# Later sequences carry one running log sum, and their decay columns go

## The chip, the cores and the metric

The kernel runs on one core of one Trainium2 chip. The metric is device time in microseconds (us). The kernel before takes 425.86 us as the median of three runs (425.14 to 426.12).

## What is computed

For 4 sequences of 768 tokens, 8 heads of 48 features, a gated linear attention runs first. A state S decays with a complex factor a(t) per feature, takes in k v', and is read by q. A gated MLP with a spatial product follows on the attention's output x.

```python
scale = np.minimum(mag, 0.999) / (mag + 1e-06)        # mag = |a|
for t in range(S):
    new_re = ar * S_re - ai * S_im
    new_im = ar * S_im + ai * S_re
    S_re, S_im = (new_re + kv, new_im)
    y[:, :, t] = np.einsum('bhd,bhde->bhe', q[:, :, t], S_re)
...
h = gelu(x @ w_in);  u, v = halves of h
v_s = np.einsum('ts,bsd->btd', w_sg, layernorm(v) * g_ln) + b_sg[None, :, None]
return x + (u * v_s) @ w_out
```

a_re is drawn from 0.85 to 0.95.

## The kernel before, in words

The attention is done in chunks of 128 tokens: 6 for each sequence, 24 in all, called a0 to a23. The decay is turned into factors on q and k: q is multiplied by exp(+half the sum of the log magnitudes since the chunk began), k by exp of minus that, and both by a cosine and a sine. Then a chunk is a masked product (weigh, L662, gives pa; causes, L672, gives am), a state product (ps, L694) and the output (py, L719 and L724). Because the sums begin anew in each chunk, the state S has to be multiplied by the chunk's whole decay when it passes to the next one: L705 in a sequence's first chunk, L707 (add) and L710 (multiply) in the later ones.

The factors are prepared for a unit of 1 or 2 chunks at a time. The first sequence (units 0 to 3) is laid out with tokens on the partitions. The three later ones (units 4 to 12, the test is `fea(n)`) have features on the partitions and use scans along the tokens. For such a unit:

- `logs` (chain g, L407) ends in two scans of 384 columns (L448 to L450). They multiply by `going`, which is 0 at each chunk's first token, so that the sum restarts there.
- `scale` (chain e, L453) makes em and ep (the exponentials), multiplies k and q, and then makes the unit's decay columns `dec`: a DVE product `cols_` (L499), six small fp32 matmuls into `pd` (L507; each is issued as two records, so a block is 12), and a copy to SBUF by `evac` (L510).
- `turns` (chain p, L518) scans the angles. Those scans already carry over from unit to unit by the small tile `left` (L536).
- `rotate` (chain r) multiplies by cosine and sine and writes to DRAM (rk, rq); `heads` (chain z) reads them back as K and Q tiles.

The MLP of a sequence has the chains n (`normal`: load x, split it into xh and xl, product pv, gelu, norm, split into vh and vl), x (`expand`: product pu) and y (`spatial`: products pvs and po). Chain w prepares weights, h and k only check input ranges, l, m and v load inputs, o sets constants up, s takes sine and cosine.

The whole order of work is written out by hand in `ORDER` (L32 to L85). A token such as `a5` runs chain a5 up to its next `yield`; `a5:2` runs two steps, one or two primes set `alt`, which chooses the engine: `evac` (L209) uses ACT without a prime and DVE with one, `ew` uses POOL with one prime, and `stoke` (L227) issues no filler matmul without a prime, one with one and more with two. Chain f runs `stoke(warm)`, so a bare f does nothing. Each engine executes its instructions in this order, and SP issues all but one of the DMAs in this order too. Steps spoken of below: a5's sixth step copies py to yp (L728), its seventh writes yp to xd in DRAM (L732); n0_3's first step loads x from there (L764).

If a range check at the end fails (`in_range`, L892, with RE_MIN at L25), `general` does everything again with a slow recurrence.

Of the kernel before, what the change touches and what calls it, by code (L numbers as in the profile page):

```python
# [18 lines left out]
P = 128  # L19
# [5 lines left out]
RE_MIN, IM_MAX = 0.7, 0.98  # L25
# [12 lines left out]
e2'' a1 z1 e1 a1 a0' g3 e2 g3 a1'' a1 s2' t3 a1 w4:2 a1 g3 s2 w7' p2 v2 s2 w4 p3 g3:2 e2:2 a0 w4 g3:2 r3 v3 z3 g3 r2
a1 e3 w7' r3 z2 r2 w9 z3:2 w1'' p3 w12:2 w9'' l4 z2 g4 e3 z2 p3 w12 a1 m3 z3 g4 w9 z2 w4 z2 p3 w4' w12 g4 z2 m3 e3 z2
e2 p3 e3' w8 z3 w12'' e3 p3'' e3' z3' z2 e3 e3' e3 g4 z3 a2 n0_0 z3' a2'' w8 a2:2 n0_0' p3 e3 a2 s3 w5 w8 a2 g4 a2' a2  # L40
a3 a2:2 a3:2 s3 a3 s3 a3'' a3 w12 w5 a3 r4'' e3 a3 r4 n0_0' n0_0 t4 w5 z4 a3 g4 n0_0 z4 w5 z4 r5'' w10 n0_0:2 z4 v5
n0_2:2 z4 z4' v4 n0_2' a3 w5 l5 n0_0 a4 z5 z4 a4'' n0_0 r5'' w10 z4 w11 e3 z5 g4 w10' p4:2 a4:2 z5 a4'' z5:4 a4 g4 m4
n0_0 a4:2' w11 g5:2 l6 p4 w14 z5 g4 a4 a5 p4 a5:2 p4 n0_0' e4 m4 a5'' w11'' l6 a5 n0_0' a4 e4:2 w5 s4 l5 n0_2' a5 p4
w15 x0_0 a5 s4:2 n0_3 e4'' e4 n0_0 x0_0 g5:2 w15 x0_0:2 r6:2 w15 r6:2 r6'' n0_0'' x0_0 w15 n0_2 r6 r6'' x0_0:2 z6 t5
n0_2 n0_3:2'' g5 p5 e4:2 z7 n0_3' x0_3 w15' w15 g5 a6 n0_2 v7 w14 n0_0 p5 v6 w14 r6 p5 g5 x0_0 w14 p5 n0_0'' n0_3
w14'' z6 n0_2'' a6:2 w14' a7 g5 n0_3 n0_2 n0_3 p5 n0_3 x0_3 n0_2' a6:2 n0_3:2 a7 f a7 s5 n0_3 z7 g6 x0_3 m5 g5 n0_3
a7'' a6:3 e5 a6:2 p5 n0_3 e5'' f e5 o1:2 a7 a6 g6 n0_3 a6 a7'' g6'' a7 m5 l7 a7'' n0_3' l7 a7 s5:2 a7 r8 n0_3' r8
n0_3'' r8'' n0_3 n0_3:2'' n0_3 r8 a7'' n0_3'' z8 a6 g6 e5:2 t6 a6 r8'' r8 g6 a7 r8 y0_0:4 x0_3 g6 r8 y0_0' y0_0:2 z9
y0_0'' p6 y0_0 y0_0' p6 g6 y0_0 l8 y0_0 p6 y0_0'' z8 z9 y0_0 y0_0' g6 g7 y0_0 a7 x0_3 y0_0:3 a8 y0_0' g7 p6 g6 v8 p6
a9 a8 g7 e6 s6'' a9 y0_0 a8 a8' a9 m6 a8 l8 a8'' a8 s6 e5 a8 a9 s6 a8 m6 e6'' v9 y0_0 a7 a8 g7 e5 r10 t7 g7 y0_0 r10  # L50
p7 r10'' p7 r10 a9 e6 a8:2 a9:2 a8 e6' x0_3 v10 y0_3 a8 e6 r10'' z10 x0_3 g7 x0_3 g7 z11 y0_3 r10 y0_0 g8 a9 y0_0 r10'
y0_0 p7 g7 y0_3 y0_0 p7 y0_0 a9 r10 e6 y0_3:2' y0_0 g7 z10 g8:2 m7 a9:2 e7 a9 y0_3 g8 a9' p7:2 y0_3 y0_3'' g8 z11 s7'
t8 y0_3 s7 y0_3'' y0_3 a10 s7 e7 a10' a10 m7 e6'' a10' e7 a10:3 a10'' a10 a11 y0_3 a9 a10 g8 r12' a10' a10 a11'' v11
a11 n1_0 a10 l9 r12 a11'' y0_3'' y0_3 r12' a10 r12 g9 e7 n1_0 g8 e7 r12 y0_3 a11 r12 y0_3 a11 n1_0 g8 n1_0:2 a11 p8
y0_3 f r12'' v12 p8 y0_3 y0_3:2' l9 g8 n1_3 g9 n1_0:2 p8 n1_0:3 y0_3 n1_0 z12 p8 y0_3 r12 m8 z12 n1_0 y0_3 p8 n1_3 z13
g9' g9 n1_3'' y0_3 s8' n1_0 g9 y0_3 e8 y0_3 e8' e8 g9 y0_3 m8 n1_3 y0_3 a12 n1_0 y0_3 p8 a12' a12 s8:2 a12' a12 a12''
n1_0:2'' l10 t9 v13 p9 k2 z13 r14 n1_0 a12 a12'' n1_0'' n1_0 r14 e8'' n1_0' e7 a12 a13' a13:2 r14 e7 x1_3:2 l10 x1_3
# [31 lines left out]
def tile_kernel(ctx: ExitStack, tc: tile.TileContext, t_q, t_k, t_re, t_im, u_q, u_k, u_re, u_im, t_v, v, q, k, f_re, f_im,  # L89
# [40 lines left out]
    def cst(shape, dt, name):  # L130
        return const.tile(shape, dt, name=name, tag=name)
# [107 lines left out]
    def others():  # L239
        nc.gpsimd.memset(going, 1.0)  # L240
        nc.gpsimd.memset(going[:, 0:MT:P], 0.0)
# [7 lines left out]
        nc.vector.tensor_reduce(out=of_head, in_=ident.rearrange("p (j h) -> p h j", h=H), axis=AX.X, op=ALU.add)  # L249

        nc.gpsimd.memset(of_place, 0.0)
        place = of_place[:, 0:2 * D].rearrange("p (a d) -> p a d", a=2)
# [154 lines left out]
    def logs(n):  # L407
# [686 lines left out]
```

## Time and profile before

| | us |
|---|---|
| median of 3 runs | 425.86 |
| span of the profiled execution, first to last instruction | 424.2 |
| PE busy | 410.3 |
| DVE busy | 347.8 |
| ACT busy | 278.5 |
| POOL busy | 161.1 |

The profiled execution has no time recorded besides its span; the median lies 1.66 us above that span. PE is the matmul engine, DVE the vector engine, ACT the scalar engine, POOL GpSimd, SP the queue that issues DMAs. A busy PE counts matmuls in flight, and successive ones overlap; so lengths of PE work are read from start to start.

### The profile page before, as it was taken

How to read it: one execution, taken by the hardware profiler on the slowest of the kernel's cores; microseconds unless marked ns; L12 is line 12 of the kernel's file. 1: busy time of each engine (PE TensorE's matmuls, PEld its weight loads, DVE VectorE, ACT ScalarE, POOL GpSimd, SP SyncE). 2: the span in 40 equal slices, each digit the busy share in tenths (PEclk: the TensorE clock that was granted, in tenths of full speed). 3: DMA queues.
4: the chain of work that ended last, by engine and by line, in shares of the span. 5: the costliest groups of instructions: out<-in, count | busy, mean ns of one | idle time of the engine just before them, and what ended most of it. 6: DMA issues, size and time to landing. Idle time of an engine off the chain costs nothing. (4 is left out here: it accounts for less than half of the span.)

```text
span 424.2 us, 10001 instructions
## 1 busy us (share of the span) xinstructions
PE 410.3 (97%) x3914; PEld 375.8 (89%) x3914; DVE 347.8 (82%) x600; ACT 278.5 (66%) x396; POOL 161.1 (38%) x218
## 2 busy tenths in 40 slices
PE   7999998989999999999899999999999999999994
PEld 5667787879899998989899998989999989899994
DVE  5999989999999989996999698797975546585482
ACT  7899998999899768876987945855830212540010
POOL 4126248265241442815274643622121255223210
PEclk9999999999999999999999999999999999999998
DMA  6778869698498888979669879889669955653531
GB/s 207 232 244 227 263 183 285 172 279 264 123 284 257 240 290 229 286 221 289 174 173 298 232 228 286 272 225 257 138 199 298 247 164 173 194 177 110 185 97 62
DMA packets 77564, 92.95 MB, mean 219 GB/s; under 512 B 10564, under 2 KB 59462, under 8 KB 77512
## 3 DMA queue, kind: packets, MB, share of 16 engines
q1 hardware_dynamic: 77368, 92.16, 73.5%
q8 instruction: 32, 0.52, 0.5%
q14 instruction: 20, 0.16, 0.1%
q10 hardware_dynamic: 144, 0.10, 0.1%
HBM read 68.64 MB, written 23.60 MB: 217 GB/s over the span
## 5 line engine op out<-in xcount | busy, mean ns | idle before, releaser
L236 PE MATMUL pvs<-wsgh,vh 128*128 128x384 f32 x192 | 65.6, 342 | 0.0
L236 PE MATMUL pvs<-wsgh,vl 128*128 128x384 f32 x192 | 65.0, 339 | 0.0
L236 PE MATMUL pvs<-wsgl,vh 128*128 128x384 f32 x192 | 64.7, 337 | 0.0
L199 ACT ACT_TABLE_LOAD x48 | 61.6, 1283 | 1.7 <-PEq L1079 0.9
L668 PE MATMUL pa<-Q,K 96*64 96x64 f32 (+1 forms) x768 | 41.4, 250 | 1.3 <-ACT csn L200 0.9
L668 PEld LDWEIGHTS pa<-Q,K 96*64 96x64 f32 x768 | 36.9, 137 | 4.2 <-issue 1.5
L719 PE MATMUL py<-am,vbuf 128*64 128x128 f32 x384 | 38.8, 275 | 0.4 <-DVE am L678 0.4
L236 PEld LDWEIGHTS pvs<-wsgh,vh 128*128 128x128 f32 x192 | 36.0, 188 | 1.2 <-issue 0.9
L236 PEld LDWEIGHTS pvs<-wsgh,vl 128*128 128x128 f32 x192 | 36.1, 188 | 0.6 <-DVE vl L225 0.5
L236 PEld LDWEIGHTS pvs<-wsgl,vh 128*128 128x128 f32 x192 | 36.1, 188 | 0.0
L678 DVE TENSOR_TENSOR am<-pa,masks 128x512 f32<-128x512 f32 x45 | 30.3, 682 | 5.6 <-PE pa L668 4.8
L724 PE MATMUL py<-Q,S 96*48 96x128 f32 x320 | 33.8, 272 | 0.0
L236 PE MATMUL pu<-xh,winh 128*128 128x384 f32 x96 | 32.8, 341 | 0.0
L850 PE MATMUL po<-gh,wouth 128*128 128x384 f32 x96 | 32.7, 341 | 0.0
L225 POOL TENSOR_TENSOR gl<-tg,gh 128x384 fp32r<-128x384 f32 x13 | 16.8, 1290 | 41.0 <-DVE gh L222 20.8
L850 PE MATMUL po<-gh,woutl 128*128 128x384 f32 x96 | 32.4, 337 | 0.0
L236 PE MATMUL pu<-xh,winl 128*128 128x384 f32 x96 | 32.4, 337 | 0.0
L850 PE MATMUL po<-gl,wouth 128*128 128x384 f32 x96 | 32.3, 337 | 0.0
L236 PE MATMUL pu<-xl,winh 128*128 128x384 f32 x96 | 32.3, 337 | 0.0
L236 PE MATMUL pv<-winh,xh 128*128 128x512 f32 x72 | 29.0, 403 | 0.5 <-ACT u__1296 L200 0.3
L236 PE MATMUL pv<-winh,xl 128*128 128x512 f32 x72 | 28.4, 395 | 0.7 <-DVE xl L225 0.7
L863 DVE SCALAR_TENSOR_TENSOR tg<-pvs,gcol,bsg 128x384 f32<-128x384 f32 x32 | 19.5, 609 | 10.8 <-PE pvs L236 10.6
(285 smaller groups left out, 1104.6 us busy)
## 6 DMA issues: line engine op xcount, KB each, us to landing
vbuf<-in_t_v_dram SPq DMA_DIRECT2D x24, 288.0 KB, 5.7
K<-rk SPq DMA_DIRECT2D x18, 384.0 KB, 5.3
Q<-rq SPq DMA_DIRECT2D x18, 384.0 KB, 7.6
x<-xd SPq DMA_DIRECT2D x9, 576.0 KB, 6.4
xd<-yp SPq DMA_DIRECT2D x48, 96.0 KB, 3.3
gr<-in_f_im_dram SPq DMA_DIRECT2D x12, 384.0 KB, 3.7
out_dram<-x SPq DMA_DIRECT2D x23, 192.0 KB, 2.8
re<-in_u_re_dram SPq DMA_DIRECT2D x9, 384.0 KB, 5.6
```

Of the source, the lines that this page charges most:

```text
L199: nc.scalar.preload_act_table_set(SETS[t])
L225: ew().tensor_tensor(out=l, in0=src, in1=h.bitcast(F32), op=ALU.subtract)
L236: nc.tensor.matmul(o, w(i), x(i), start=(i == 0 and j == 0), stop=(i == n - 1 and j == 2))
L668: nc.tensor.matmul(pa[rows, hh, j:], K(h)[:, j:j + KB], Q(h)[:, j:], start=True, stop=True)
L678: nc.vector.tensor_tensor(out=pairs(am), in0=pairs(pa), in1=causal, op=ALU.mult)
L719: nc.tensor.matmul(py[64 * e:64 * e + 64, p_, :], Vy(h)[:, 0:64], ams[h // 4][:, h % 4, :], start=True, stop=c == 0)
L724: nc.tensor.matmul(py[64 * e:64 * e + D, p_, :], Sb()[:, h, :], Q(h), start=False, stop=True)
L850: nc.tensor.matmul(po[d], w[:, f, ds], g[:, f, :], start=f == 0 and j == 0, stop=f == NF - 1 and j == 2)
L863: nc.vector.scalar_tensor_tensor(out=tg, in0=pv, scalar=gcol[:, f:f + 1], in1=bsg[:, tsl], op0=ALU.mult, op1=ALU.add)
```

## The change

- The range check's lower bound RE_MIN becomes 0.845.
- In the later sequences the sums run on through the whole sequence. Three scans of 256 columns, one for each feature tile, begin at the unit before's last value (`total`), or at 128.0 in the first unit. `total` is a small DVE instruction, twice for each later sequence.
- With that S needs no decay between chunks: the first chunk's S is a plain copy by `evac`, the next ones' only the add. `cols_`, the matmuls into `pd` and the copy to `dec` go, and their steps stay as empty ones.
- The constants `going`, `of_head` and `of_place` go.
- ORDER loses its 69 bare f tokens, and 39 steps move. Four steps change their primes: n0_2's and n0_3's fourth steps lose one (one `stoke` less each), a4's seventh step (S multiply) loses one, a10's thirteenth (copy to yp) gets one.

```diff
-RE_MIN, IM_MAX = 0.7, 0.98
+RE_MIN, IM_MAX = 0.845, 0.98
+MIDDLE = 128.0
...
-        for j in range(0, NK * UT, MT):
-            x = fl(U[n]["lo"])[:, j:j + MT]
-            nc.vector.tensor_tensor_scan(out=x, data0=going, data1=x, initial=0.0, op0=ALU.mult, op1=ALU.add)
+        b, c0, m = units[n]
+        for kt in range(NK):
+            x = U[n]["lo"][:, kt, :]
+            nc.vector.tensor_tensor_scan(out=x, data0=x, data1=x, initial=run["sum", b, c0][:, kt:kt + 1] if c0 else MIDDLE,
+                                         op0=ALU.add, op1=ALU.bypass)
+        if c0 + m < NCH:
+            total = run["sum", b, c0 + m] = gp.tile([P, NK], F32, tag="sum", name="sum", bufs=2)
+            ends = U[n]["lo"][:, :, m * P - 1]
+            nc.vector.tensor_tensor(out=total, in0=ends, in1=ends, op=ALU.max)
...
+        if fea(n):
+            yield
+            psm.tile([P, DM], F32, tag="m", name="pd")
+            yield
+            yield
+            return
...
-        cols_ = gp.tile([P, NK, UC, H], F32, tag="sq", name="cols_", bufs=1)
-        nc.vector.tensor_tensor(out=cols_[:, :, 0:m],
...
-                nc.tensor.matmul(pd[r, 0:m, :], of_place[:, j + r.start:j + r.stop], cols_[:, kt, 0:m, :],
...
-        evac(dec[:, 0:m], pd[0:2 * D, 0:m])
...
-            if c == 0:
+            if fea(n):
+                if c == 0:
+                    evac(Sn, ps[0:2 * D])
+                else:
+                    nc.vector.tensor_tensor(out=Sn, in0=ps[0:2 * D], in1=Sb(), op=ALU.add)
+                    yield
+            elif c == 0:
```

Three of the moved places, with steps numbered by # and the f tokens left out (before, then after):

```diff
-n0_2#4' a5#6 p4#6 w15#1 x0_0#1 a5#7 s4#2 s4#3 n0_3#1
+n0_2#4 p4#6 w15#1 x0_0#1 s4#2 s4#3 a5#6 a5#7 n0_3#1
...
-y0_3#17 r12#7'' v12#1 p8#2 ... l9#2 g8#9 n1_3#1 ... z12#1 p8#4 y0_3#22 r12#8 m8#1 z12#2
+y0_3#17 g8#9 v12#1 r12#7'' p8#2 ... n1_3#1 ... l9#2 ... z12#1 p8#4 p8#5 y0_3#22 m8#1 r12#8 z12#2
...
-n1_3#4 y0_3#28 a12#1 n1_0#14 y0_3#29 p8#6 a12#2'
+y0_3#28 a12#1 n1_0#14 y0_3#29 n1_3#4 a12#2'
```

## Rows read from the trace of the kernel before

**Rows 1.** The page: busy time, share of the span, instructions of each engine.
```profile
PE 410.3 (97%) x3914; PEld 375.8 (89%) x3914; DVE 347.8 (82%) x600; ACT 278.5 (66%) x396; POOL 161.1 (38%) x218
```

**Rows 2.** PE's waits: for whom, us in total, times, longest.
```profile
PE pk L650 <- ACT yp L213: 1.1, 1, 1.1
PE pk L620 <- ACT Q L213: 1.1, 1, 1.1
...
PE pv L236 <- DVE xl L225: 0.7, 1, 0.7
PE ps L694 <- DVE kt L211: 0.4, 1, 0.4
...
PE pv L236 <- ACT u__1296 L200: 0.3, 1, 0.3
```

**Rows 3.** Busy time by window: PE, PEld, DVE, ACT, POOL, then PEclk, DMA share, GB/s.
```profile
80.00:90.00 10.00, 9.49 (x58) 8.15 (x56) 9.75 (x15) 9.91 (x13) 2.89 (x4) 1.00 0.89 257
```

**Rows 4.** The chain that ended last: start us, us, what.
```profile
327.51 0.12 DVE cols__4374 L499
...
333.45 6.62 DMA Q<-rq
...
340.20 0.85 PE pa L668 x12
```

**Rows 5.** PE's timeline: start us, us, line, what, idle before and its releaser.
```profile
87.60 0.52 PE L507 MATMUL pd<-cols__1151,of_place 128*64 128x16 f32 x12
...
128.70 0.47 PE L507 MATMUL pd<-cols__1546,of_place 128*64 128x16 f32 x12
129.02 0.76 PE L694 MATMUL ps<-vbuf,kt 128*33 128x48 f32 x22
...
181.02 1.14 PE L694 MATMUL ps<-vbuf,kt 128*64 128x48 f32 x32 [0.45 <-DVE kt L211]
```

**Rows 6.** Scans by line (min/median/max ns, first and last start).
```profile
L450 DVE TENSOR_TENSOR_SCAN lo<-going,lo x18: 924/948/2541, 72.9 to 299.2; 128x384 f32<-128x384 f32 x18
L524 DVE TENSOR_TENSOR_SCAN im<-im,left x18: 719/745/934, 90.1 to 283.8; 128x256 f32<-128x256 f32 x18
```

**Rows 7.** Instructions on tile dec from 85 to 345 us, in the same columns.
```profile
L710 DVE TENSOR_TENSOR S<-S,dec x8: 524/550/2204, 111.1 to 315.7; 96x384 f32<-96x384 f32 x8
...
L710 POOL TENSOR_TENSOR S<-S,dec x4: 874/1276/1477, 156.1 to 341.0; 96x384 f32<-96x384 f32 x4
```

**Rows 8.** ACT's timeline around a5's copy to yp.
```profile
78.69 0.59 ACT L213 COPY yp<-py 128x512 f32<-128x512 f32 x1
79.30 1.28 ACT L199 ACT_TABLE_LOAD   x1
...
81.34 0.92 ACT L200 ACTIVATE csn<-csn,cols 128x768 f32<-128x768 f32 x1
```

**Rows 9.** SP's timeline: n0_3's three loads of x.
```profile
80.17 3.24 SPq L764 DMA_DIRECT2D x<-xd  x3
```

**Rows 10.** Tile x from 60 to 100 us: landing of its loads.
```profile
DMA to landing us min/median/max: 3.6/3.7/3.8
```

**Rows 11.** DVE's timeline: n0_3's xh, xl; unit 7's q; a wait near the end.
```profile
88.08 0.76 DVE L222 CAST xh<-x 128x1152 fp32r<-128x1152 f32 x1
88.87 1.36 DVE L225 TENSOR_TENSOR xl<-x,xh 128x1152 fp32r<-128x1152 f32 x1
...
165.46 0.95 DVE L604 TENSOR_TENSOR q<-q,csn 128x768 f32<-128x768 f32 x1
...
326.49 0.56 DVE L883 TENSOR_TENSOR x<-po,x 128x384 f32<-128x384 f32 x1 [3.09 <-PE po L850]
```

**Rows 12.** SP's and PE's timelines: chunk 12's Q and its first use.
```profile
166.88 0.91 SPq L607 DMA_DIRECT2D rq<-q  x2
...
173.57 0.34 SPq L628 DMA_DIRECT2D Q<-rq  x1
...
178.71 1.56 PE L668 MATMUL pa<-Q,K 96*64 96x128 f32 x32
```

More of the change, by code (lines that the diff above doesn't have):

```diff
@@ L38 @@
[L38 to L57, printed above, removed]
@@ new lines @@
+w11 e3 z5 g4 w10' p4:2 a4:2 z5 a4'' z5 a4 z5:3 g4 m4 n0_0 a4 a4' w11 g5:2 l6 p4 w14 z5 g4 a4 a5 p4 a5:2 p4 n0_0' e4 m4
+a5'' w11'' l6 a5 n0_0' a4 e4:2 w5 s4 l5 n0_2 p4 w15 x0_0 s4:2 a5:2 n0_3 e4'' e4 n0_0 x0_0 g5:2 w15 x0_0:2 r6 w15 r6:3
+r6'' x0_0 n0_2 w15 r6 r6'' x0_0:2 z6 t5 n0_2 n0_3:2'' g5 p5 e4:2 z7 n0_3 x0_3 g5 w15' w15 n0_0'' a6 p5 n0_2 v7 w14
+n0_0 v6 w14 r6 p5 g5 x0_3 x0_0 w14 p5 n0_0'' n0_3 w14'' z6 n0_2'' a6:2 w14' a7 g5 n0_3 n0_2 n0_3 p5 n0_3 n0_2' a6:2
+n0_3:2 a7:2 s5 n0_3 z7 g6 x0_3 m5 g5 n0_3 a7'' a6:2 g6 a6 e5 a6:2 p5 n0_3 e5'' e5 o1:2 a7 a6 n0_3 a6 a7'' g6'' a7 m5
@@ new lines @@
+l7 a7'' n0_3' l7 a7 s5:2 a7 r8 n0_3' r8 n0_3'' r8'' n0_3 n0_3:2'' n0_3 r8 a7'' n0_3'' z8 a6 g6 e5:2 t6 a6 r8'' r8 g6
+a7 r8 y0_0:4 x0_3 g6 r8 y0_0' y0_0:2 z9 y0_0'' p6 y0_0 y0_0' p6 g6 y0_0 l8 y0_0 p6 y0_0'' z8 z9 y0_0 y0_0' g6 g7 y0_0
+a7 x0_3 y0_0:3 a8 y0_0' g7 p6 g6 v8 p6 a9 a8 g7 e6 s6'' a9 y0_0 a8 a8' a9 m6 a8 l8 a8'' a8 s6 e5 a8 a9 s6 a8 m6 e6''
+v9 y0_0 a7 a8 g7 e5 r10 t7 g7 y0_0 r10 p7 r10'' p7 r10 a9 e6 a8:2 a9:2 a8 e6' x0_3 v10 y0_3 a8 e6 r10'' z10 x0_3 g7
+x0_3 g7 z11 y0_3 r10 y0_0 g8 a9 y0_0 r10' y0_0 p7 g7 y0_3 y0_0 p7 y0_0 a9 r10 e6 y0_3:2' y0_0 g7 z10 g8:2 m7 a9:2 e7
@@ new lines @@
+a13' a13:2 r14 e7 x1_3:2 l10 x1_3 e8 x1_3 r14 n1_0 r14'' r14 n1_3:6 z15 x1_3 n1_0' n1_3:2 x1_3 a12 m9 a12 a13'' a13
+a12 a13:2 a13'' a13:2 a13'' r14' n1_3 g9 r14 n1_3' z14 e8:2 n1_3 n1_3' n1_3'' a13 n1_3 a15' n1_3'' a13 n1_3:2 g9 n1_3
+p9:2 x1_3 y1_3 x1_0 v14 g10 a13 g10:2 y1_3 p9 a15 g10 x1_3 g10 z15 g9 y1_3 e9 y1_3:2' y1_3 a12 y1_3 y1_3'' y1_3 p9
+y1_3' g10 y1_3 x1_0 a14 e9'' z14 x1_0' a14'' a14 a15 a14' a14:2 v15 a15' e9 y1_3 s9 m9 a14 l11 a14'' g10 s9 a12 a14:2
+a14' a15 e9'' a14 l11 a15 s9 y1_3' r16 e9 r16 r16'' y1_3' r16:2 a15 x1_0 t10 p10:3 g10 y1_3 r16 k2 x1_0:5 a14' x1_0
@@ new lines @@
+n2_0:2 m11 n2_0 z19 t12 y1_0 p11 n2_0 s11:2 r20' a18 a18' a18 y1_0 h20 p12 a17 v18 y1_0:2 n2_3 e11'' y1_0:2 n2_0' n2_0
+a18 n2_0 y1_0 n2_0'' p12 a19' a19 n2_0 n2_0' a19 a18 h11 a18 a19 a18 y1_0 a18 r20 n2_0'' a18:2 a19 n2_3 r20' a18 a19''
+a19 e11 h10 a19:2 n2_3 h11 r20 a19 r20'' n2_0'' h10 a19:2 a18 n2_3:2 v20 n2_3 z20 n2_0'' r20 p12 m12 a18 n2_3 r20'
+n2_3:2 p12 r20 y1_0 n2_3:2 x2_3:2 k8 x2_3 n2_3 z21 n2_3 x2_3 n2_3 h20 n2_3 x2_3 n2_3'' x2_0 p12 n2_3' n2_3:3'' x2_3
+n2_3 n2_3'' x2_3 x2_0 k8 s12 y2_3:2 a21 h8 y2_3 x2_3 g12 a21 x2_0'' y2_3'' a21 g12 y2_3' a21 e12 y2_3:3 z21 y2_3
@@ new lines @@
+y2_3'' y2_3:2 z20 y2_3 a19' y2_3'' k5 y2_3'' e12 h4 y2_3 x2_0 k5 e12 a20:2' a20 v21 a20' h8 a20 s12 a20 a19 a20 e11
+s12 h15 h4 a20 h1 a20 a21 e11'' r22' r22:3 a20 y2_3 z23 a20'' a20 a21' a21:2 y2_3'' a21 h15 h22 a21 y2_3'' a21:2
+x2_0:2 h5 m12 y2_3'' h22 h0 x2_0 y2_3 e12' y2_3 v23 z22 y2_0 h5' v22 y2_3 h2 a20' y2_0 x2_0 y2_3:3 y2_0'' e12 r22:3
+x2_0 r22 y2_3 x2_0 y2_3 a20 y2_0 y2_0'' a21 z22 y2_0:2 k7 y2_0:2' y2_0:2 z23 y2_0 a21 h0' a22:5 a22' a22 e12 h2' a22:2
+x2_0 a23 y2_0 a22 y2_3 h18 e12'' a22' a22 y2_0'' n3_0 a23:2 a23'' a22 n3_0' y2_0 a22 a23 n3_0' y2_0:2 a23:2 y2_0' n3_0
@@ new lines @@
+h18 n3_0:2 k10 h1' k10 n3_0:3 y2_0'' y2_0 n3_3 n3_0 n3_3 k7 n3_0 y2_0:2 n3_0 n3_3' h7 h7'' k12 y2_0:3 n3_0 k1 n3_0'
+y2_0 n3_0' y2_0 n3_0 y2_0 n3_3 n3_0' n3_0:2 n3_3 n3_0' n3_3 n3_0 n3_3 k12 n3_0 h6 n3_3:3 x3_3 n3_3 x3_3 n3_3 y2_0
+x3_3:3 h19 x3_3 k1 x3_3 n3_3:2 n3_3' x3_0 h19 n3_3 n3_3:2' n3_3'' x3_3 h13 n3_3' n3_3'' n3_3 h23 k6 h13 x3_0:2 h6 h23
+y3_3:2 y3_3:3'' y3_3:2 y3_3' y3_3:5 k6 k9 y3_3'' h14 y3_3' h14 y3_3 k4 k0 x3_0 y3_0 y3_3 y3_0 k3 x3_0 k4 y3_3' x3_0
+y3_3'' k9 y3_3' h12 y3_3:3 y3_0' k3 h12 y3_3:2 x3_0 y3_3:2 h21:2 y3_3 h16 h17 x3_0 y3_0'' h17 y3_0' y3_0:2 x3_0 y3_0''
@@ L85 @@
+y3_3 y3_0' k0 k11 y3_0 h3 h16 y3_0 ok x3_0 h3 y3_0 y3_0'' k11 ok y3_0 x3_0 y3_0 ok:2 y3_0:2 ok y3_0:3 ok y3_0:3 ok
+y3_0:9
 """
@@ L248, in others @@
                                     base=g0 + KB - P, pattern=[[1, P]], channel_multiplier=-1)
-        nc.vector.tensor_reduce(out=of_head, in_=ident.rearrange("p (j h) -> p h j", h=H), axis=AX.X, op=ALU.add)
-        nc.gpsimd.memset(of_place, 0.0)
-        place = of_place[:, 0:2 * D].rearrange("p (a d) -> p a d", a=2)
-        nc.gpsimd.memset(place, 1.0)
-        nc.gpsimd.affine_select(out=place, in_=place, compare_op=ALU.is_ge, fill=0.0,
-                                base=H * 2 * DG, pattern=[[0, 2], [-H, D]], channel_multiplier=1)
-        nc.gpsimd.affine_select(out=place, in_=place, compare_op=ALU.is_ge, fill=0.0,
-                                base=H - 1 - H * 2 * DG, pattern=[[0, 2], [H, D]], channel_multiplier=-1)
         yield
@@ L485, in scale @@
             yield
-        dec = ap_.tile([2 * D, UC, H], F32, tag="dec", name="dec", bufs=2)
-        if not fea(n):
-            row = dram.tile([UC, DM], F32, name=f"row{n}")
-            nc.sync.dma_start(out=row[0:m].rearrange("(o c) f -> o c f", o=1), in_=ep[P - 1:P, 0:m])
+        if fea(n):
             yield
-            for a in range(2):
-                with nc.allow_non_contiguous_dma(reason="one row becomes columns"):
-                    nc.sync.dma_start(out=dec[a * D:(a + 1) * D, 0:m, :], in_=row[0:m].rearrange("c (h d) -> d c h", d=D))
-            U[n]["dec"] = dec
+            psm.tile([P, DM], F32, tag="m", name="pd")
+            yield
             yield
             return
-        cols_ = gp.tile([P, NK, UC, H], F32, tag="sq", name="cols_", bufs=1)
-        nc.vector.tensor_tensor(out=cols_[:, :, 0:m],
-                                in0=ep[:, :, P - 1:m * P:P].unsqueeze(3).broadcast_to([P, NK, m, H]),
-                                in1=of_head.unsqueeze(1).unsqueeze(1).broadcast_to([P, NK, m, H]), op=ALU.mult)
+        dec = ap_.tile([2 * D, UC, H], F32, tag="dec", name="dec", bufs=2)
+        row = dram.tile([UC, DM], F32, name=f"row{n}")
+        nc.sync.dma_start(out=row[0:m].rearrange("(o c) f -> o c f", o=1), in_=ep[P - 1:P, 0:m])
         yield
-        pd = psm.tile([2 * D + 1, UC, H], F32, tag="m", name="pd")
-        for kt in range(NK):
-            j = (NK - 1 - kt) * DG
-            for r in COLS:
-                nc.tensor.matmul(pd[r, 0:m, :], of_place[:, j + r.start:j + r.stop], cols_[:, kt, 0:m, :],
-                                 start=kt == 0, stop=kt == NK - 1)
-        yield
-        evac(dec[:, 0:m], pd[0:2 * D, 0:m])
+        for a in range(2):
+            with nc.allow_non_contiguous_dma(reason="one row becomes columns"):
+                nc.sync.dma_start(out=dec[a * D:(a + 1) * D, 0:m, :], in_=row[0:m].rearrange("c (h d) -> d c h", d=D))
         U[n]["dec"] = dec
```

57 lines of the change are left out of this document (19 added, 38 removed).

## The prediction

> **What bounds the kernel now.** I read the page first, then PE's waits, the busy time by windows, the chain that ended last, and the timelines of the places that the change touches. The page gives PE busy for 97% of the span, DVE for 82%, and ACT and POOL less [rows 1]. The list of PE's waits is short [rows 2]: inside the run the longest single one is 1.1 us, and the five rows shown make up 3.6 us. So time goes where PE works less, and whatever makes PE wait costs its full length. But one stretch is different. From 80 to 90 us DVE is busy for 9.75 of 10 us and ACT for 9.91, and PE is the one that has gaps [rows 3]. There PE follows the other two, and PE work taken out before it only makes a wait longer. The chain that ended last [rows 4] runs back from PE's last stretch over a read of Q (6.62 us) to DVE at 327.51, so near the end PE hangs on a DMA for a moment.
>
> **The blocks of pd.** A block of 12 small matmuls starts at 128.70 and the next work at 129.02 [rows 5]: 0.32 us of PE. The block at 87.60 is busy for 0.52; that is the upper bound, and 0.32, read from start to start on a PE that doesn't wait, is the value. There are nine. Three of them don't pay. The first (87.60) stands ahead of the wait for xl. Unit 7's is followed by PE's wait of 0.45 for kt at 181.02. Unit 12's comes shortly ahead of the wait for Q that ends at 340.20. The other six give 6 x 0.32 = **1.9 us** (up to 3.1 at 0.52).
>
> **The end.** In front of that Q stands `cols_` on DVE at 327.51, 0.12 us and some issue. DVE itself had waited 3.09 us for PE's po just before, at 326.49 [rows 11], so the chain to Q moves up with PE, and by `cols_` more: **0.2 us** gained (0 to 0.3).
>
> **Scans and S on DVE and POOL.** The old scans are 18 x 0.948 = 17.1 us, the new ones have the shape of those for the angles, 27 x 0.745 = 20.1 us [rows 6]: 3.0 us more. The six `total` have no row of their own; they read three columns, so between 0.1 (as `cols_`) and 0.6 (an S multiply) each, 0.1 taken for their size. Out go DVE's eight S multiplies at 0.55 (4.4 us), the same in three first chunks (1.7 us, which ACT's copy takes over: a copy of yp, somewhat larger, is 0.59 [rows 8]) and nine `cols_` (1.1 us). Two steps come to DVE by their primes, about 0.55 each. Net: 3.0 + 0.6 + 1.1 - 4.4 - 1.7 - 1.1 = 2.5 us less on DVE, spread over 270 us, and on POOL four multiplies of 1.28 less [rows 7]. PE feels this only where it waits for DVE or for what follows DVE: behind 95 us that is 0.4 (kt) and 1.1 (yp) [rows 2]. I take a third, **0.5 us** (0 to 1.5).
>
> **Where the order is moved: x of chunk 5.** a5's copy to yp now stands behind ACT's two sine steps. Before it ran at 78.69; then came a table load at 79.30 and the sines, ending at 82.26 [rows 8]. Moved behind them it ends 2.96 us later. Behind it on SP stand its own two writes, the three loads of x (80.17 to 83.41 [rows 9]), and all of unit 4's writes and reads of K and Q. The last load lands some 3.7 us after its issue [rows 10], so by 87.1, and xh starts at 88.08 [rows 11]: 1.0 us of slack. Up to 2.0 us of delay reach xh, xl and PE's pv. Against it, a4's first product now stands behind the transposes, which brings ACT's Q copies forward; PE's wait for one of them is 1.1 us [rows 2], so ACT may be that much ahead and 0.9 is left. The next wait, 0.3 for ACT's u, would shrink by as much. I take **0.6 us lost**, between 0 and 2.0. What PE saves ahead of this place (the first pd block, two fillers, the wait for Q) I put at nothing: the wait for xl covers it. Without that cover it would be worth 1.1 + 0.32 and the fillers.
>
> **Chunk 12's Q.** Unit 7's q multiply (165.46 [rows 11]) now stands behind three scans, 2.2 us, and its write behind a load of k. The write at 166.88 was read back only at 173.57, and PE used Q at 178.71 without a wait [rows 12]. Half of the 2.2 us, 1.1, may reach PE; of that, 0.45 and 0.32 (the wait for kt and the block of pd that no longer stands in front of it) are lost there anyway. So 0.3 if Q had landed just in time, 0 if it had slack: **0.1 us lost** (0 to 3.2). The other moved steps pass each other within a microsecond or two on engines that don't wait there; between -0.5 and +0.5, taken as 0. The constants at the start run beside PE's wait for the first inputs and give nothing. The bare f tokens issue nothing.
>
> **Sum.** -1.9 - 0.2 - 0.5 + 0.6 + 0.1 = -1.9 us. Against the profiled span this is 424.2 - 1.9 = 422.3; the median lies 1.66 us above that span, and I keep this distance: 425.86 - 1.9 = **424.0 us**.
>
> **A rule weighed against a row.** The old scan takes 0.948 us at the median, but up to 2.541 [rows 6], and an S multiply on DVE 2.204 in place of 0.55 [rows 7]. So DVE is at times held by something that isn't in its own queue. The Trainium skill, SBUF — State Buffer, section "SBUF: two separate sides", says that a DVE operation with two SBUF inputs and a GpSimd operation that reads SBUF take the shared port for their whole length, the one that comes second waiting. That speaks against the change, since there are nine more scans to be caught; it is the last rival below.
>
> **Rivals.**
> 1. All of it pays: x of chunk 5 lands in time and DVE keeps up. Then nine blocks count (2.9 us), PE's wait for ACT's Q goes (1.1), and the relief is 0.5: 425.86 - 4.5 = 421.4. For it: PE is at 97%. Against: DVE and ACT are full from 80 to 90 us, so PE can't go ahead of them. Chance 0.20.
> 2. The gain is given back at chunk 5's x: the whole 2.0 us of delay reaches PE and no relief shows. -1.9 - 0.2 + 2.0 + 0.1 = 0.0: 425.9. For it: ACT has no gap in which to be ahead. Against: the wait for Q that the order removes. Chance 0.15.
> 3. Slower: PE waits for chunk 12's Q. If two of the scans ahead of its q multiply are held to 2.5 us, as the longest was, and the k load takes its part, Q comes some 4.0 us later; less 0.77 lost there anyway that is 3.2 us in place of 0.1: -1.9 + 3.1 = +1.2, 427.1. It decides once Q lands more than 2.8 us later (1.9 + 0.1 + 0.77), if it had no slack. For it: the 6.7 us from write to read-back show a full DMA queue. Against: a queue that is full delays the write less than its issue moves. Chance 0.13.
> 4. The carried scans are held by POOL: one more scan held by 1.6 us (2.541 - 0.948) ahead of a wait of PE: 425.6. By that page's rule this is what to expect of every scan that starts beside a POOL operation; the median of 0.948 says that most don't. Chance 0.07.
>
> That the change does not do what it says would mean the slow recurrence after a failed check; inputs from 0.85 up pass 0.845, so no chance is set aside.
>
> **How the numbers follow.** The forecast has 0.45; its own range, from the term's bounds, is 423.0 to 425.0. A measurement of this kernel can tell about 0.2% (0.85 us) from no change. Forecast and rival 1 are faster, 0.65; rivals 2 and 4 are the same, 0.21 after rounding; rival 3 is slower, 0.14. The range reaches down to rival 1's centre and up short of rival 3's: 421.2 to 426.2.
>
> **What would show it.** Right: no pd block on PE; PE's waits after 130 us no longer in total; last work on DVE ahead of Q is PE-bound still; the copy to yp of chunk 5 near 82 us and xh near 89. Wrong: xh before 88 with PE's pv earlier by over 1 us (rival 1); pv past 92 (rival 2); a wait of PE for Q near 178 us (rival 3); scans of 256 columns over 1.5 us on the way to a wait of PE (rival 4). If PE's matmuls themselves got slower or faster, the whole argument would be wrong.

## The result: slower by 0.6 to 0.9%, and the profile after

| | before | changed | ratio (95%) |
|---|---|---|---|
| median, first chip | 425.58 us (5 runs) | 429.33 us (5 runs, 427.04 to 434.47) | 1.0088 (1.0060 to 1.0117) |
| median, measured again with the experiments | 425.90 us (35 runs) | 428.26 us (12 runs) | 1.0058 (1.0033 to 1.0082) |
| span of the profiled execution | 424.2 us | 427.2 us (its own time 428.99) | |

Ratios leave out runs in a slower state, one of the changed kernel's first five (434.47 us) among them. Forecast were 424.0 us and a range up to 426.2. PE works less, as forecast, and so do DVE and POOL. The page after, as [rows 1]:

```profile
PE 409.0 (96%) x3802; PEld 373.2 (87%) x3802; DVE 343.2 (80%) x592; ACT 279.4 (65%) x393; POOL 150.0 (35%) x207
```

All three engines that got relief lost busy time while the span grew by 3.0 us. So the time is in waits and, as shown below, in a lower clock. PE's waits after (for whom, us in total, times, longest), as [rows 2]:

```profile
PE pa L647 <- DMA Q<-rq: 1.7, 3, 0.9
PE pk L599 <- DVE S L692: 1.4, 1, 1.4
...
PE pv L231 <- DVE xh L217: 1.3, 1, 1.3
PE pk L629 <- DVE kt L206: 1.2, 1, 1.2
PE pk L629 <- DMA K<-rk: 0.8, 2, 0.6
...
PE pv L231 <- DVE xl L220: 0.6, 1, 0.6
```

Two of these lie behind one another at 88.5 to 91.1 us (xh, xl), and three at 181.5 to 185.5 us (Q, K, kt). Busy time by window after, with the columns of [rows 3]; first the ten microseconds of [rows 3], then two places in detail:

```profile
80.00:90.00 10.00, 8.73 (x46) 7.77 (x45) 9.86 (x17) 9.60 (x13) 2.21 (x4) 1.00 0.66 190
...
88.00:90.00 2.00, 0.73 (x4) 0.44 (x3) 1.86 (x4) 1.97 (x3) 1.37 (x4) 1.00 1.09 325
90.00:92.00 2.00, 1.40 (x4) 0.82 (x4) 1.78 (x3) 1.99 (x3) 1.05 (x1) 0.78 1.01 288
92.00:94.00 2.00, 2.00 (x6) 1.59 (x5) 2.00 (x4) 1.97 (x3) 1.18 (x2) 0.50 1.05 271
...
184.00:186.00 2.00, 0.78 (x9) 0.59 (x8) 2.00 (x6) 2.00 (x4) 0.00 (x0) 1.00 0.42 158
186.00:188.00 2.00, 2.00 (x10) 2.00 (x10) 1.97 (x4) 1.98 (x3) 0.00 (x0) 0.68 0.94 280
188.00:190.00 2.00, 2.00 (x8) 2.00 (x7) 2.00 (x4) 0.80 (x2) 0.00 (x0) 0.50 0.92 287
```

Read the columns PE and PEclk together. PE is busy for 0.73 of 2 us, and then the granted clock falls to 0.50, its 1.2 GHz level. In the kernel before it was 1.00 in both places:

```profile
90.00:100.00 10.00, 9.40 (x52) 8.05 (x53) 9.76 (x19) 9.46 (x17) 6.91 (x10) 1.00 0.89 244
180.00:190.00 10.00, 9.55 (x95) 8.50 (x91) 9.90 (x16) 7.41 (x12) 2.10 (x4) 1.00 0.76 234
```

The price is in PE's timeline after:

```profile
187.19 0.52 PE L231 MATMUL pu<-xh,winh 128*128 128x384 f32 x1
187.51 0.52 PE L231 MATMUL pu<-xl,winh 128*128 128x384 f32 x1
...
190.27 0.34 PE L231 MATMUL pu<-xl,winh 128*128 128x384 f32 x1
190.45 0.34 PE L231 MATMUL pu<-xh,winl 128*128 128x384 f32 x1
```

At the lower level pu matmuls start every 0.32 us, at the full one every 0.18. Ten of them between 186.87 and 190.07 us cost some 1.4 us.

The chain that ended last now runs through the second place (start us, us, what; a stretch of it):

```profile
166.12 3.45 DMA xd<-yp
...
170.06 5.42 DMA im<-in_u_im_dram
...
175.62 2.03 POOL im L401
...
180.68 0.83 ACT l L195
...
181.53 2.54 DVE l L425
...
185.00 0.93 DVE kt L206 x2
```

That is the load of im for unit 9 (the second step of chain l9), which the new order puts behind the load of x. By the chain, x is issued only when yp has been written, 166.12 + 3.45 us, and im stands behind it on SP. SP's timeline, first before, then after:

```profile
164.78 0.45 SPq L375 DMA_DIRECT2D im<-in_u_im_dram  x1
165.88 0.38 SPq L764 DMA_DIRECT2D x<-xd  x1
```

```profile
169.63 0.38 SPq L749 DMA_DIRECT2D x<-xd  x1
170.06 0.48 SPq L359 DMA_DIRECT2D im<-in_u_im_dram  x1
```

Of the 5.28 us between the two issues, some 2.7 are a lag that PE already has at 172 us; the rest is the move. Who waited is in the timelines of POOL, ACT and DVE after (the bracket is the idle time before):

```profile
175.62 2.02 POOL L401 TENSOR_TENSOR im<-im,inv 128x768 f32<-128x768 f32 x1 [2.19 <-DMA im<-in_u_im_dram]
177.67 0.85 ACT L195 ACTIVATE l<-im 128x768 f32<-128x768 f32 x1 [1.75 <-POOL im L401]
181.45 1.81 POOL L469 TENSOR_TENSOR k<-k,em 128x768 f32<-128x768 f32 x1
181.53 2.54 DVE L425 SCALAR_TENSOR_TENSOR l<-re,l 128x768 f32<-128x768 f32 x1 [1.67 <-ACT l L195]
```

DVE's l takes 2.54 us in place of 0.96: it starts at 181.53, and POOL's k multiply runs from 181.45 to 183.26. The copies of kt come behind it, and PE's 1.22 us of waiting for them.

### The profile page after: what moved, and what is told of

The parts are those of the page before. It is cut to its first block, busy times and chain, and to the rows that moved or that the text cites. A ratio compares the mean times of both kernels' runs of the same rounds, so it can differ in the third digit from the quotient of the medians.

```text
span 427.2 us, 9750 instructions
## 1 busy us (share of the span) xinstructions
PE 409.0 (96%) x3802; PEld 373.2 (87%) x3802; DVE 343.2 (80%) x592; ACT 279.4 (65%) x393; POOL 150.0 (35%) x207
## 4 chain that ended last, share of the span: by engine, by line
PE 45%; DVE 17%; ACT 12%; DMA 12%; issue 5%; POOL 5%; SPq 2%; DVEq 0%; ACTq 0%; POOLq 0%
PE pvs L231 16%; PE po L835 7%; PE pv L231 6%; PE pu L231 6%; PE pa L647 3%; ACT L194 3%; DMA xd<-yp 3%; ACT l L195 2%; DMA vbuf<-in_t_v_dram 2%; PE py L704 2%; DMA x<-xd 2%; PE py L709 2%; DVE lo L435 2%; DVE am L657 2%; PE ps L673 1%
## 5 line engine op out<-in xcount | busy, mean ns | idle before, releaser
L231 PE MATMUL pv<-winh,xl 128*128 128x512 f32 x72 | 29.4, 408 | 0.6 <-DVE xl L220 0.6
L231 PE MATMUL pv<-winl,xh 128*128 128x512 f32 x72 | 28.9, 402 | 0.0
```

The source lines that it names most:

```text
L231: nc.tensor.matmul(o, w(i), x(i), start=(i == 0 and j == 0), stop=(i == n - 1 and j == 2))
```

## The experiments

Each kernel ran in five rounds beside the kernel before on the same chip, most with 12 runs; ratios are to it. Their intervals are 0.15 to 0.3% wide on each side, so 1 us is about the least that one kernel of this study settles. The kernels ran in five groups, on four chips; those of two groups are compared only through the kernel before. In the diffs a step is written as its chain and number, as in the change above.

| kernel | sums | first place | second place | ratio (95%) |
|---|---|---|---|---|
| sums_old_order | new | old | old | 1.0021 (1.0000 to 1.0042) |
| new_order_alone | old | new | new | 1.0015 (0.9991 to 1.0039) |
| second_place_moved | new | old | new | 1.0032 (1.0002 to 1.0061) |
| first_place_moved | new | new | old | 1.0049 (1.0022 to 1.0075) |
| early_sums | new in sequence 2 | old | old | 0.9981 (0.9967 to 0.9995) |
| late_sums | new in 3 and 4 | old | old | 1.0040 (1.0016 to 1.0063) |
| two_fillers | new | new, 2 fillers | new | 1.0087 (1.0070 to 1.0103) |
| load_of_im_back | new | new | new, load old | 1.0032 (1.0010 to 1.0054) |
| scan_apart | new | old | old, scans earlier | 1.0000 (0.9979 to 1.0021) |
| three_steps_back | new | new, yp old | new, load old | 1.0027 (1.0004 to 1.0051) |
| second_place_load_back | new | old | new, load old | 0.9994 (0.9965 to 1.0023) |
| first_place_front | new | front new | new, load old | 0.9997 (0.9976 to 1.0018) |
| first_place_rear | new | rear new | new, load old | 1.0026 (0.9999 to 1.0053) |
| fillers_kept | new | new, fillers old | new, load old | 1.0042 (1.0015 to 1.0069) |
| q_ahead | new | old | new, load and q old | 1.0019 (0.9994 to 1.0044) |
| rear_last_three | new | last 3 of rear new | new, load old | 1.0010 (0.9986 to 1.0034) |
| front_and_scan_apart | new | front new | old, scans earlier | 1.0005 (0.9990 to 1.0020) |

### Sums or order

Theory 1: the new sums gain what was forecast, and the moved steps lose more, as PE now waits in two places and the clock falls behind each. Theory 2: the order is innocent, and the carried scans and the plain copy of S cost more than the dec blocks did. Four kernels part them: the order of before under the new sums, the new order under the old sums, and the new sums with either group of moves alone.

```diff
 the changed kernel, its ORDER in the first place (sums_old_order has both groups so)
-n0_2#4 p4#6 w15#1 x0_0#1 s4#2 s4#3 a5#6 a5#7 n0_3#1
+n0_2#4' a5#6 p4#6 w15#1 x0_0#1 a5#7 s4#2 s4#3 n0_3#1
...
```

> The change's new sums and recurrence, with the order of before (the 39 moved steps back in their old places, the four turned primes and the two fillers of chunk 5 as before). Theory 1: the new sums gain what the forecast said and the moved steps lose it, so this is faster than the kernel before: 422 to 424 us, and the granted clock stays at 1.00 from 90 to 100 us and from 180 to 190 us. Theory 2: the carried scans and the copy of S on ACT cost more than the dec blocks did, whatever the order: 427 us or more.

> The kernel before, with the changed order alone (39 moved steps, turned primes, two fillers less; the blocks of pd, cols_ and the old scans stay). Theory 1: slower than before by what the order costs, 428 to 432 us, with PE waiting near 72, 90 and 185 us and the granted clock down in one or both of 90 to 100 and 180 to 190 us. Theory 2: within 0.5 us of the kernel before.

> The new sums, with the order of before up to chunk 7 and the moved steps of the first sequence's second half alone (the second place, 160 to 200 us). Theory 1, the loss split between the two places, some 2 us and a fall of the clock each: 425 to 427 us, clock 1.00 from 90 to 100 us and below 0.9 from 180 to 190 us. If the second place carries all of the loss: as the changed kernel, 428 or more. Theory 2: within 0.5 us of the new sums with the old order.

> The new sums, with the moved steps of the first place alone (60 to 115 us: the turned primes, the two fillers less and chunk 5's yp copy behind the sines among them) and the order of before from there on. Theory 1, the loss split between the two places: 425 to 427 us, clock below 0.9 from 90 to 100 us and 1.00 from 180 to 190 us. If the first place carries all of the loss: 428 or more. Theory 2: within 0.5 us of the new sums with the old order.

Neither theory held. The sums with the old order are not faster but slower by 0.21%, an interval that just touches no change. On top of them the first place costs 0.28 more and the second 0.11, together 0.60%, where the changed kernel measured 0.58 and 0.88. But under the old sums the whole order costs 0.15%, and that interval includes no change. So what the order costs seems to depend on the sums beside it. And there is no gain from the sums themselves. One place where they lose is in DVE's timeline with the old order:

```profile
169.38 2.95 DVE L435 TENSOR_TENSOR_SCAN lo<-lo,sum 128x256 f32<-128x256 f32 x3
172.37 1.63 DVE L440 TENSOR_TENSOR sum<-lo 128x3 f32<-128x3 f32 x1
```

and in POOL's of the same kernel:

```profile
170.53 1.26 POOL L220 TENSOR_TENSOR gl<-tg,gh 128x384 fp32r<-128x384 f32 x1
171.75 2.23 POOL L401 TENSOR_TENSOR im<-im,inv 128x768 f32<-128x768 f32 x1
```

`sum` reads three columns and took 0.16 us in all six places of the changed kernel. Here it takes 1.63 and ends at 174.00, POOL's multiply at 173.98. The Trainium skill, SBUF — State Buffer, section "SBUF: two separate sides", says that of a DVE instruction with two SBUF inputs and a GpSimd one that reads SBUF the second waits for the whole of the first; this row agrees, to 0.02 us. Before, the two old scans stood in this place for 2.06 us and ended at 169.49, ahead of the multiply.

To see what that is worth, each PE instruction is matched with the same one before; the difference is PE's lag. In this profile it grows by 1.5 us between 174 and 182 us. It grows by 1.5 at 126 us too, where PE waits 1.28 us for K, a DMA. That second loss has no explanation here: early_sums, below, waits 0.60 in that place, and the changed kernel not at all.

### Which sequence's sums

```diff
 the kernel before; carried(n) chooses the new scans, no dec block and the plain S
+def carried(n):
+    return units[n][0] == 1        # early_sums; late_sums: units[n][0] > 1
```

> The kernel before with its old order; the new sums for the second sequence alone (units 4 to 6), old sums and dec blocks for the third and fourth. Theory A: up to some 220 us DVE's queue is full and sets the pace, so PE work taken out there only turns into waits, and the new sums lose there by what their scans are held beside POOL's wide multiplies: 1 to 2.5 us slower than before. Theory B (the new sums cost a little everywhere, by their longer chain on DVE): 0.3 us slower, a third of what all of them cost with the old order.

> The kernel before with its old order; the new sums for the third and fourth sequences alone (units 7 to 12). Theory A: from some 220 us on PE sets the pace, so that the six dec blocks pay their 0.32 us each, as the forecast had it: 1 to 2 us faster than before (424 to 425 where before has 426). Theory B: 0.3 to 0.6 us slower than before.

Theory A was wrong in both signs, and so was B for the early ones. The second sequence's sums gain 0.2%, the later ones lose 0.4%, and their sum is again what all of them cost (0.21). The reason is the place where the third sequence begins: its unit 8 is prepared at 168 us, while the second sequence is still in work. DVE's timeline of late_sums has the same held pair as above:

```profile
168.27 2.95 DVE L455 TENSOR_TENSOR_SCAN lo<-lo,sum 128x256 f32<-128x256 f32 x3
171.25 1.63 DVE L460 TENSOR_TENSOR sum<-lo 128x3 f32<-128x3 f32 x1
```

In PE's lag, late_sums falls 2.3 us behind between 174 and 181 us and wins back 1.3 from 200 to the end. early_sums falls 1.0 behind by 200 us and ends 0.6 behind; that its median is lower all the same is told under the last heading.

### The load of im, and the fillers

```diff
 load_of_im_back: the changed kernel
-y0_3#20' n1_3#1 n1_0#6 ... y0_3#21 l9#2 n1_0#11
+y0_3#20' l9#2 n1_3#1 n1_0#6 ... y0_3#21 n1_0#11
...
 two_fillers: the changed kernel
-n0_3#4
+n0_3#4''        # with "most" 2 in place of 20 for this chunk
```

> The changed kernel with two filler matmuls (0.70 us each in the kernel before) ahead of chunk 5's first pv, where PE idled for 1.27 us and then for 0.60; nothing else. They delay nothing, or 0.1 us, as PE waits there for xh. Theory A (PE's idling there lets the granted clock fall, and the fall is what costs): the clock stays at 1.00 from 90 to 96 us, and the median is 1 to 2 us below the changed kernel's. Theory B (the clock falls for another reason, or costs nothing since PE follows DVE there): within 0.5 us of the changed kernel.

> The changed kernel with one step put back: unit 9's load of im ahead of the store of x, as before, so that it is issued near 165 us in place of 170. Theory A (its late landing holds POOL's im multiply 2.2 us, ACT's and DVE's l and so the copies of kt, and PE idles before 185.5): POOL's multiply before 173 us, PE's waits from 181 to 186 us under 0.7 us together in place of 1.98, the clock at 1.00 from 186 to 192 us: 1.5 to 3 us less than the changed kernel. Theory B (the queue of DMAs is full there and the loads only change places): within 0.5 us of the changed kernel.

One step put back takes 1.0088 and 1.0058 down to 1.0032. SP's and POOL's timelines of load_of_im_back show theory A's first link:

```profile
165.68 1.78 SPq L364 DMA_DIRECT2D vbuf<-in_t_v_dram  x1
167.51 0.43 SPq L359 DMA_DIRECT2D im<-in_u_im_dram  x1
...
172.40 2.24 POOL L401 TENSOR_TENSOR im<-im,inv 128x768 f32<-128x768 f32 x1
```

The issue is 2.55 us earlier than in the changed kernel (1.0 of it a smaller lag of the whole), POOL's multiply 3.2 us and without a wait. There is no wait for kt any more; one of 0.77 for Q and one of 0.21 for K are left, and the clock is 1.00 from 180 to 190 us. (From 90 to 100 us it still falls, to 0.83.)

The late load alone is not enough, though. It is late in new_order_alone (issued at 168.72) and in second_place_moved (169.45) too. There POOL's im multiply waits for ACT in the one and 1.13 us for im in the other, and DVE's l takes 0.95 and 0.94 us, for it runs from 179.96 and 180.80, and POOL's k multiply starts only at 182.02 and 182.86. From 172 to 210 us PE's lag shrinks by 0.3 and 0.5 us in these two. It grows by 1.3, 1.3 and 1.7 in the changed kernel, its repeat and two_fillers, where l is held for 2.54 to 2.56 us, and shrinks by 1.0 in load_of_im_back. In these profiles the late load costs where it makes l meet that multiply.

The fillers did what they were to do (clock 1.00 from 90 to 100 us) and brought nothing that can be measured. That profile is of the slowest of their seven runs, with a wait of 2.50 us at 56 us, and the clock fell at 50 to 60 us (0.83) and at 190 to 200 us (0.84) instead. So keeping PE's clock up at 90 us brings nothing that shows; whether the first place costs anything by its clock, these runs don't say.

### The held scans, and the repeat

```diff
 scan_apart: the new sums with the old order
-y0_3#17 r12#7'' v12#1 ... l9#2 g8#9 n1_3#1
+y0_3#17 r12#7'' g8#9 v12#1 ... l9#2 n1_3#1
```

> All new sums with the order of before, and one step moved: unit 8's carried scans stand behind unit 7's q multiply, five steps earlier, and so no longer beside POOL's im multiply. Theory A (the held scans and the copy of their ends, 2.95 and 1.63 us in place of 2.0 and 0.16 with the old order, are the loss of the late sums): the copy of the ends takes 0.2 us, PE's waits for xl near 179 and kt near 185 shrink to under 1 us together, and the median is 1.5 to 2.5 us below the new sums with the old order: 424.3 to 425.3, faster than before. Theory B (POOL's multiply then meets another instruction of DVE, which is held as long): within 0.5 us of the new sums with the old order.

> The changed kernel once more, unaltered, on the chip of these runs. Theory A: 428.5 to 430, and the profile shows again PE's waits before 91 and 185.5 us and a granted clock below 0.9 in both stretches behind them. Theory B (the falls of the clock are chance): the clock is 1.00 in at least one of them with the same waits ahead of it.

> The changed kernel with three steps put back: the load of im of unit 9 as before, and the copy and the writes of chunk 5's yp ahead of ACT's two sine steps as before. Theory A (the yp copy behind the sines delays the loads of x and the writes of K and Q behind them on SP by 2.4 us, and PE waits for K near 97 us or, earlier, for xh): 0.5 to 1.5 us below the changed kernel with the load alone put back, so 425.8 to 426.8, and no wait for K near 97 us. Theory B (the x loads had slack, and PE follows DVE's xh there): within 0.4 us of the load alone put back.

> All new sums, the order of before up to chunk 7, the second place's moved steps without the move of unit 9's load of im. Theory A: 1 to 2.5 us below the second place alone: 425 to 426.5, with PE's waits from 178 to 190 us under 1 us and the clock 1.00 there. Theory B: as the second place alone, 427.5 or more.

scan_apart's DVE shows the pair released:

```profile
166.98 2.03 DVE L435 TENSOR_TENSOR_SCAN lo<-lo,sum 128x256 f32<-128x256 f32 x3
169.04 0.16 DVE L440 TENSOR_TENSOR sum<-lo 128x3 f32<-128x3 f32 x1
...
171.05 1.52 DVE L503 TENSOR_TENSOR_SCAN im<-im,left 128x256 f32<-128x256 f32 x1
```

2.4 us less for the pair (2.95 + 1.63 against 2.03 + 0.16), of which 0.8 returns: POOL's multiply, from 171.98, now catches a scan of the angles (1.52 in place of 0.74). The ratio goes from 1.0021 to 1.0000, so A's mechanism is there in the trace, but at 0.9 us, with intervals that overlap, it is half of what A gave it, and the kernel only draws level. The wait for xl near 179 is gone, that for kt is 0.73.

The repeat of the changed kernel has the same waits in the same places, but not the same clock:

```profile
90.00:100.00 10.00, 8.54 (x44) 6.75 (x45) 9.65 (x16) 9.93 (x15) 5.24 (x9) 1.00 0.85 246
180.00:190.00 10.00, 7.99 (x65) 7.36 (x64) 8.94 (x14) 8.22 (x11) 2.56 (x7) 0.83 0.82 285
```

PE idled for 1.39 us before xh and 0.59 before xl, more than the first time, and the clock stayed at 1.00 there. For the first stretch theory B holds: whether the clock falls after such idling differs from run to run.

With the yp copy of chunk 5 put back too (three_steps_back) there is no wait for K near 97 us, but load_of_im_back, its comparison, has none in its profile either. The time did not change beyond the intervals: B. Leaving the first place as before and putting the load back (second_place_load_back) gives 0.9994 against 1.0032, a price of 0.4% again, though here the intervals overlap. The profiles don't show it: this one has PE waiting 1.93 us for Q, and the clock at 0.66 from 180 to 190 us.

### What the first place costs

```diff
 q_ahead: second_place_load_back
-y0_3#17 g8#9 v12#1 r12#7'' p8#2
+y0_3#17 v12#1 r12#7'' g8#9 p8#2
```

Of the others, first_place_front takes the first place's moves up to a4's seventh step (the S multiply) and first_place_rear those from n0_2's fourth step (chunk 2's pv) on; fillers_kept takes all with the two fillers, rear_last_three only p5#2, x0_3#2 and g6#2; front_and_scan_apart joins the front with scan_apart.

> All new sums, the second place's moves with unit 9's load of im as before, and of the first place only the steps moved in its front part (the rotation of chunk 3 to the copy of chunk 4's yp, 55 to 78 us). Theory A (the front is what the first place costs: S of chunk 4 comes late and PE waits 1.2 to 1.4 us for it near 72 us): as with the whole first place, 426.8 to 427.5. Theory B (the rear costs): as without the first place, 425.3 to 426.2.

> As the run before, with only the rear part of the first place's moves (chunk 5's yp copy behind the sines, the two fillers gone, unit 4's rotation and the copies behind it, 78 to 115 us). Theory A (the front costs): 425.3 to 426.2. Theory B (the rear costs, by PE's idling before xh and xl and what follows it): 426.8 to 427.5, and more runs with the mean clock below 0.998.

> All moved steps of both places but unit 9's load of im, and the two fillers of chunk 5 kept as before. If the fillers' going is what the first place costs: 425.3 to 426.2, the clock 1.00 from 90 to 100 us. If it is the moved steps: 426.8 to 427.5, as with the load of im alone put back.

> All new sums, first place as before, second place's moves with unit 9's load of im as before, and unit 7's q multiply put back ahead of unit 8's scans. Theory A (the q multiply behind the scans makes chunk 12's Q late, 1.93 us of PE's wait near 182 us in the profile without this): no wait for Q near 182, and 0.5 to 1.5 us below the kernel without this move: 424.3 to 425.3, faster than before. Theory B (Q waits for the queue of DMAs, not for the multiply): within 0.4 us of it.

> All new sums, first place as before but for the last three steps moved in its rear part (a scan of unit 5's angles, the second block of pu of chunks 3 to 5, the im multiply of unit 6), second place's moves with unit 9's load of im as before. If these three carry what the rear costs: 1.0025 or more times the kernel before. If the steps ahead of them do (the copy and normalization of chunk 1's values on ACT, chunk 2's gelu, with the yp copy of chunk 5 and the fillers among them): 0.9985 to 1.001 times the kernel before.

> The candidate that beats both: all new sums, the front part of the first place's moves, the order of before from there on but for unit 8's scans, which stand behind unit 7's q multiply. Theory A (the held scans, the rear of the first place and the load of im are all that the change loses by): the six dec blocks behind 200 us pay, 424 to 425 us, 0.996 to 0.999 times the kernel before, with the mean clock at 0.998 or more in most runs. Theory B: within 0.1% of the kernel before.

Only taken together do these tell something. With the load put back, the four kernels that have the rear's moves measure 1.0026, 1.0027, 1.0032 and 1.0042, a mean of 1.0032; the three without them 0.9994, 0.9997 and 1.0019, a mean of 1.0003. So the rear costs some 0.3% (give or take 0.2), 1.2 us, and the front and the two fillers nothing that shows. PE's lag agrees: between 84 and 112 us it grows by 0.7 to 1.5 us in the eight profiles with all new sums and the rear, by 0.4 to 0.5 in seven without, and by 0.8 in second_place_moved, where the clock fell. (The front brings the longest new wait of the list, 1.4 us for S at 72 us. It is 1.38 in first_place_front too, and costs nothing there.) Within the rear, the yp copy shows nothing by itself, and the last three moves alone (1.0010) lie between. Which step it is stays open.

q_ahead took the wait for Q near 182 us away that the kernel without it had in its profile:

```profile
182.11 2.18 PE L647 MATMUL pa<-Q,K 96*64 96x128 f32 x24 [1.93 <-DMA Q<-rq]
```

and brought no gain (1.0019 against 0.9994): B. Still, the wait goes with the move: of the 12 profiles with the q multiply moved, 9 show PE waiting there for this Q, 0.18 to 1.93 us, and of the 8 others one does (early_sums, 0.41). What that is worth lies within the intervals.

front_and_scan_apart leaves out all that was found and draws level with the kernel before (0.9990 to 1.0020); theory B. So even without these losses the forecast 1.9 us, a ratio of 0.9955, don't appear, and why not stays open. The only kernel that beats both is early_sums, by 0.8 us.

## Why the prediction was wrong

**The step that failed** is "The other moved steps pass each other within a microsecond or two on engines that don't wait there; between -0.5 and +0.5, taken as 0." One of them, unit 9's load of im, went behind the load of x on SP (164.78 us before, 170.06 after, about half of it by the move), and behind it stood POOL, then ACT, then DVE, then PE. With the rear's moves and the new sums, the kernels with the load late measure 1.0088, 1.0058 and 1.0087, and load_of_im_back 1.0032: 0.46% (give or take 0.26), 1.9 us. With the old sums no such price was measured (the whole order, load late, 1.0015). The rear of the first place costs another 1.2 us, by which of its steps stays open. The prediction followed the yp copy and the q multiply to the end of their chains, and no other moved step, though the trace of before would have told the load's: POOL took up im at 170.27 us without a wait, 5.5 us after its issue.

**The blocks of pd.** Where PE sets the pace their size was right. From 205 to 415 us the new sums with the old order win 1.6 us on the kernel before (3.6 us behind, then 2.0); four blocks of 0.32 (unit 12's among them, which the prediction left out) and the 0.2 of the end give 1.5. What was lost ahead of that is more than the rest of the 1.9 us.

**Scans and S.** The new scans take 20.0 us, as forecast (20.1). The old ones were put at 18 medians, 17.1 us; DVE's list (busy us, mean ns), before and, under it, after, has 20.5:

```profile
L450 DVE TENSOR_TENSOR_SCAN lo<-going,lo 128x384 f32<-128x384 f32 x18 | 20.5, 1176 | 0.0
```

```profile
L435 DVE TENSOR_TENSOR_SCAN lo<-lo,sum 128x256 f32<-128x256 f32 x18 | 13.6, 809 | 0.0
L435 DVE TENSOR_TENSOR_SCAN lo<-lo 128x256 f32<-128x256 f32 x9 | 6.4, 762 | 0.0
```

So they are 0.5 us less together, not 3.0 more, and the nine `cols_` were 4.4 us, not 1.1. DVE loses 4.6 us in place of 2.5, and would have lost more if others had not got longer, l by 2.4 and gl by 2.0. Yet with the old order the "relief" of 0.5 us had the wrong sign. What counts is not how long DVE works but when one instruction stands beside a wide one of POOL. This was rival 4, with a chance of 0.07 and one scan of 1.6 us; it was a pair of 2.4 us on the way to PE's xl and kt, and took the sums with the old order from the forecast gain towards a loss. The changed order avoids just this pair (167.52, 2.02 us, and 0.16 for `sum`), and meets another at l, 2.54 us.

**x of chunk 5.** The signs came: the yp copy at 82.66 (forecast near 82), xh at 88.85 (near 89). The second was luck. DVE has no idle time ahead of xh, before or after, so it did not wait for x; it was some 0.7 us late in all it did there, and with the copy put back xh starts no earlier (88.07 us in three_steps_back, 88.02 in load_of_im_back). The price of 0.6 us cannot be told from 0.

**Chunk 12's Q.** Rival 3 had the right side, slower, and asked for PE to wait near 178 us. PE waited 0.51 us, until 181.97, and in most profiles with this move it waits there; but putting the q multiply back gave no time. The rival is not shown to be what made the kernel slower, and 0.1 for this term is neither confirmed nor refuted.

**The waits after 130 us** were to be no longer in total: those of over 0.15 us went from 1.9 to 4.3 us (3.9 in the repeat).

**The range** of 423.0 to 425.0 does not come from the bounds of the terms. Added up, these reach from 420.5 to 429.7, and the measured time lies inside.

**The fillers**, costed at nothing, are nothing within the interval. **The clock** was no term at all. In the runs beside each other, the mean granted clock was 0.998 or more in 24 of 34 of the kernel before and in 1 of 12 of the changed one. Over the runs that the ratios count, those of a kernel with a mean clock lower by 0.01 were some 3 us longer (an estimate by a line through 363 runs). The changed kernel's mean is 0.004 lower than that of the kernel before, so about 1.2 of the 2.5 us between their means goes with the clock. The fall at 186 us cost some 1.4 us; that makes a wait of 1 to 2 us worth twice its length when the clock does fall.

## What to carry to other kernels

A moved step has to be followed through every engine that waits for it, DMA issues first: the load's issue takes 0.5 us anywhere on its queue, and what its place is worth shows four engines further on. Before moving or lengthening work on DVE, lay POOL's wide two-input instructions beside it by their times; a three-column instruction that meets one can last until the wide one ends (1.63 us in place of 0.16). Work taken off an engine pays only where that engine isn't about to wait for another, so count it by stretches, not by the span. And cost a group of instructions by its summed time: 18 times the median was 17.1 us, the sum 20.5.

## What was not expected

**The end.** From ACT's issue of the last write to the end of the span are 4.89 us before and 5.03 with the order alone, and 3.63 to 4.01 in the 18 other profiles, whichever sequences carry their sums. That last write lands sooner (name, queue, KB, us to landing); before and, under it, changed:

```profile
out_dram<-x ACTq DMA_DIRECT2D x1, 96.0 KB, 3.5
```

```profile
out_dram<-x ACTq DMA_DIRECT2D x1, 96.0 KB, 2.3
```

So every kernel with new sums wins about 1 us at the end by none of the terms, and the body of the changed kernel, by its profile, loses 4.2 us, not 3.0. early_sums, 0.6 us behind at its last stretch of PE, is faster by this alone in its profile, one execution. In the two with the longer end a packet of the instruction queue q8 falls into the same microsecond as this write, in early_sums and in the changed kernel 1 to 2 us ahead of it; whether that is the cause wasn't tried.

**The clock's fall** follows, in the changed kernel, idling in pieces (1.27 and 0.60 us; 0.51, 0.25 and 1.22), with a little work between them, and in its repeat it did not follow 1.39 and 0.59. In second_place_load_back it follows one piece of 1.93 us.
